# Retention outputs of a block in two TensorE visits instead of three, the last product in two halves, and one chunk's load ahead of a queue of stores

## The chip, the cores and the metric

One core of a Trainium2 chip runs the whole program. The metric is the time of one execution on the device in microseconds (us), lower is better; a second view is one profiled execution, whose trace gives every instruction's start and duration on TensorE (PE; its weight loads PEld), VectorE (DVE), ScalarE (ACT), GpSimd (POOL) and the DMA queue that SyncE issues (SP).

## The reference

Retention with a decay per head, and behind it a feed-forward layer with ELU:

```python
for t in range(S):                       # B, H, S, D = 4, 8, 768, 64
    state = gamma * state + einsum('bhd,bhe->bhde', k[:, :, t], v[:, :, t])
    y[:, :, t] = scale * einsum('bhd,bhde->bhe', q[:, :, t], state)
x = y.transpose(0, 2, 1, 3).reshape(B * S, H * D)        # 3072 x 512
h = x @ w_in                                             # 512 x 2048
out = where(h > 0, h, exp(min(h, 0)) - 1) @ w_out        # 2048 x 512
```

All of it is float32.

## The kernel before, in words

**Blocks and chunks.** The 3072 tokens are 24 chunks of 128, six to a sequence, and six blocks of 512 tokens (four chunks, two pairs of chunks). Block 0 (tb 0) is computed plainly, block 1 with Strassen's seven products once or twice, blocks 2 and 3 together and then 4 and 5 together ("big", `nb` 0 and 1) with two or three levels. The feed-forward layer of one group is on TensorE while the retention of the next is done between its products, in *visits*: `retention_step(tb, step)` is called at places written out by hand, steps 0 to 4 for a block. The schedule is manual: every engine runs its instructions in the order in which the program issues them.

**A block's retention.** Step 0 is `scores` of both pairs: k^T q in 64 x 64 matmuls (line 331), then a mask on DVE (line 342) into the chunk's tile. Step 1 is `states`: k^T v' (line 371), then a chain of running sums on DVE (line 383). Steps 2 to 4 are `outputs_step`, which drives one generator `outputs(tb, pp)` for each pair of chunks: `within` (line 427) is the masked scores times v', `across` (line 442) the state times q, both added up in PSUM tiles `y`; then DVE multiplies by the decay into x (line 417). `y` of a pair is two tiles of 512 columns, one for each half (64 tokens) of a chunk; a tile is written by matmuls from the lower and the upper 64 rows of the array. So that these do not overlap, DVE copies a few elements of it (`seen`, line 411) between `across(other=0)` and `across(other=1)`, and TensorE waits for that copy.

With two generators the three steps run: step 2, pair 0 as far as its `seen`; step 3, the end of pair 0 and pair 1 as far as its `seen`; step 4, the end of pair 1 (blocks 1 to 3). For blocks 4 and 5 the ends of both pairs are in step 4. Scores, k^T v' and `y` tiles share the four buffers of pool `ps_r`, each one PSUM bank.

**Where the visits are.** Block 1: between the plain products of block 0 (line 557). Block 2: in `first(3)` and `second_twice(1)` (lines 784 and 978). Block 3: pair 0's scores and states in `second_twice(1)`; pair 1's scores and states and the output steps in the first two of eight `big_twice` units of `nb` 0 (line 1286), in five visits. Blocks 4 and 5: in `second_big(0)` (line 1395), at the places of the list `VISITS`, named by (product number, "first", "middle" or "end").

**Loads and stores.** All DMAs are issued by SP in program order. A chunk is 1 MB, `load(m)` (line 125), into one of four buffers; `scale_v` (line 305) then multiplies v by the decay on POOL. Weights come through a ring of slots `wq` (line 854): `done` frees a slot behind the last product that read it and `fetch` issues the next loads of a long list; pieces named in `blocked` are held until `sent(j)`. Block 3's last chunk (15) is loaded at (5, "end") of `second_twice(1)`, behind six of eight stores of weight sums `xb` (line 679) that are issued from step 5 on; `sent(1)` follows at (6, "first").

**The last product.** `inner_end` (line 1435 on) is the seven small products of the last of seven; its product 3 adds onto the bank `pa` of products 1, 6 and 5, and a DVE add and one store (lines 1466 and 1467) end the program:

```python
            product(j, 3, pa, False)
            add(res[:, 0, 1], pa, k[:, 0, 1])
            nc.sync.dma_start(to[:, 0, 1], res[:, 0, 1])
```

Of the kernel before, what the change touches and what calls it, by code (L numbers as in the profile page):

```python
# [28 lines left out]
def kernel(  # L29
# [40 lines left out]
    C = P  # L70
# [376 lines left out]
    def outputs_of_first():  # L447

        y = [bank(x).rearrange("p a (b x d) -> p (a b) x d", b=2, x=2) for x in "bd"]
        for x in range(2):  # L450
# [19 lines left out]
            if not x:  # L470
                yield

    def outputs_step(tb, step):

        if step == 0:
            held["y"] = [outputs(tb, pp) for pp in range(2)]
        early_end = tb <= 3
        if step and early_end:
            next(held["y"][step - 1], None)
        elif step == 2:  # L480
            for g in held["y"]:
                next(g, None)
        if step < 2:
            next(held["y"][step])
            next(held["y"][step])

    half = [slice(0, TH), slice(TH, TB)]

# [356 lines left out]
    def sent(j):  # L845
        send_small()
        blocked.discard((2, "t", j))
        fetch()
# [531 lines left out]
    def second_big(nb, behind_last):  # L1380
        ts, kept2 = {}, {}
        ends = nb == NB - 1

        def input_parts(j):
            x = INPUT2[j]
            t = (slots_e, slots_s)[len(ts) % 2]
            b11, b12, b21, b22 = (quarter(x, a, b) for a in range(2) for b in range(2))
            yield from quarters_of(t, b11, b12, b21, b22, nc.gpsimd if j == 1 else nc.vector)
            ts[j] = {1: b11, 2: b21, 3: b22, 4: t[3], 5: t[0], 6: t[1], 7: t[2]}

        def product(j, k, ps, begin):
            name = (nb + 2, j, k)
            w = where[name].rearrange("p (f d) -> p f d", f=4)
            for f in range(4):
                nc.tensor.matmul(  # L1395
                    ps, lhsT=w[:, f, :], rhs=ts[j][k][:, f // 2, f % 2, :], start=(begin and f == 0), stop=(f == 3),
                    skip_group_check=True,
                )
            done(name)

        def copy(ps):
            m = small.tile([P, TH], FP32, name="ms", tag="ms")
            nc.scalar.copy(m, ps)  # L1403
            return m

        def add(o, x, y):
            nc.vector.tensor_tensor(out=o, in0=x, in1=y, op=ALU.add)  # L1407

        part = lambda x: bank(x)[:, 0]

        def inner(j):
            res = (two if j in (6, 7) else mpool).tile([P, 2, 2, TH], FP32, name="res", tag="m")
            pa = part("a")
            product(j, 1, pa, True)
            m1 = copy(pa)
            pb = part("b")
            product(j, 2, pb, True)
            add(res[:, 0, 0], pb, m1)
            yield
            product(j, 6, pa, False)  # L1420
            u2 = copy(pa)
            pd = part("d")
            product(j, 7, pd, True)
            yield
            product(j, 5, pa, False)
            add(res[:, 1, 1], pd, copy(pa))
            yield
            product(j, 3, pa, False)
            nc.scalar.copy(res[:, 0, 1], pa)  # L1429
            yield  # L1430
            product(j, 4, pd, False)
            add(res[:, 1, 0], pd, u2)
            sum_up(j, res.rearrange("p d t c -> p (d t c)"))

        def inner_end(j):

            res = mpool.tile([P, 2, 2, TH], FP32, name="res", tag="m")
            to = out_of[nb][1, 0].rearrange("p (d t c) -> p d t c", d=2, t=2)
            k = kept2[6].rearrange("p (d t c) -> p d t c", d=2, t=2)
            pa = part("a")  # L1440
            product(j, 1, pa, True)
            m1 = copy(pa)
            pb = part("b")
            product(j, 2, pb, True)
            add(res[:, 0, 0], pb, m1)
            yield
            product(j, 6, pa, False)
            u2 = copy(pa)
            pd = part("d")
            product(j, 7, pd, True)  # L1450
            m7 = copy(pd)
            yield
            add(u2, u2, k[:, 1, 0])
            add(u2, pd, u2)
            product(j, 5, pa, False)
            add(res[:, 1, 1], pa, m7)
            yield
            add(res[:, 0, 0], res[:, 0, 0], k[:, 0, 0])
            nc.sync.dma_start(to[:, 0, 0], res[:, 0, 0])
            add(res[:, 1, 1], res[:, 1, 1], k[:, 1, 1])  # L1460
            pb = part("b")
            product(j, 4, pb, True)
            add(res[:, 1, 0], pb, u2)
            nc.sync.dma_start(to[:, 1], res[:, 1])
            product(j, 3, pa, False)
            add(res[:, 0, 1], pa, k[:, 0, 1])
            nc.sync.dma_start(to[:, 0, 1], res[:, 0, 1])

        def store(name, h):
            nc.sync.dma_start(out_of[nb][int(name[1]) - 1, int(name[2]) - 1], h)  # L1470

        def sum_up(j, m):

            kept2[j] = m
            if j == 2:
                add(m, kept2[1], m)
                store("C11", m)
            elif j == 6:
                add(m, kept2[1], m)
            elif j == 5:  # L1480
                add(m, kept2[6], m)
                add(kept2[6], kept2[6], kept2[7])
                add(kept2[7], m, kept2[7])
                store("C22", kept2[7])
                add(kept2[3], m, kept2[3])
                store("C12", kept2[3])
            elif j == 4:
                add(m, kept2[6], m)
                store("C21", m)

        for _ in input_parts(1):
            yield "input"
        yield "inputs"
        before = iter(())
        changes = itertools.chain(*(next_big_input(x) for x in ("T3", "T2", "T1", "T4")))
        for at, j in enumerate(BIG2):
            cur = (inner_end if j == 4 and ends else inner)(j)
            next(cur)
            if j == 1:
                yield "tail"  # L1500
            for _ in before:
                pass
            if at:
                yield "first"
            some(changes, {2: 1, 3: 4, 7: 1, 5: 2}.get(j, 0))
            parts = input_parts(BIG2[at + 1]) if at + 1 < 7 else iter(())
            if j == 1:

                next(cur)
                yield "elu"  # L1510
                some(parts, 2)
            else:
                some(parts, 2)
                if at == 6:
                    behind_last()
                next(cur)
                yield "middle"
            next(cur)
            if j != 1:
                for _ in parts:  # L1520
                    pass
                some(changes, {2: 2, 6: 3, 7: 2}.get(j, 0))
            before = cur
            yield j
            if j == 1:
                for _ in parts:
                    pass
                some(changes, 1)
        for _ in before:
            yield "rest"  # L1530
# [267 lines left out]
    flush()  # L1798
    retention_step(2, 2)
    step, VISITS = 0, {(1, "first"): 3, (1, "end"): 4}  # L1800
    LOADS = {(1, "first"): 0, (1, "end"): 1, (3, "end"): 2, (5, "end"): 3}
    for s in sec:
        if s == "first":
            step += 1
        at = (step, s if s in ("first", "middle") else "end")
        if s in ORDER2 and 1 <= step <= 4:
            some(smalls[1], 1 if step < 4 else 3)
        if step == 5:
            send_small(2)
        elif at == (6, "first"):  # L1810
            sent(1)
        if at in VISITS:
            retention_step(2, VISITS[at])
        if at in LOADS:
            load(3 * CPB + LOADS[at])
            scale_v(3 * CPB + LOADS[at])
        if at == (3, "first"):
            scores(3, 0)
        elif at == (4, "first"):
            states(3, 0)  # L1820
        if s == ORDER2[-1]:
            break
    for _ in sec:
        pass
    mid.close()
# [5 lines left out]
    for nb in range(NB):  # L1831
# [83 lines left out]
        for at, (j, sub) in enumerate(ORDER1):  # L1915
# [18 lines left out]
            if nb == 0:  # L1934
                if at == 0:
                    scores(3, 1)
                elif at == 1:
                    retention_step(3, 3)
            if at == 7:
                run(tail)  # L1940
                seeds(0, 1, first=True)
            next(cur)
            tail = cur
            if nb == 0:
                if at == 0:
                    states(3, 1)
                elif at == 1:
                    retention_step(3, 4)
                    run(tail)
            side(at, 2)  # L1950
# [81 lines left out]
        if more:  # L2032
# [1 line left out]
                scale_v(groups[0] * CPB + n)  # L2034
        step = 0
        VISITS = [
            (0, "end"), (1, "end"), (2, "middle"), (2, "end"), (3, "middle"),
            (5, "first"), (5, "end"), (6, "first"), (6, "middle"), (6, "end"),
        ]
        LOADS = [(3, "middle"), (3, "end"), (4, "first"), (4, "middle")]  # L2040
# [70 lines left out]
```

## Time and profile before

| | us |
|---|---|
| three runs | 612.51, 608.03, 608.09 (median 608.09) |
| the profiled execution | 607.38 |
| its span from the first to the last instruction | 605.6 |
| PE busy in the span | 599.0 (99%) |
| PEld, DVE, ACT, POOL busy | 491.9, 508.6, 261.5, 98.3 |
| granted TensorE clock | 1.00 |
| DMA share of 16 engines | 70.9%, 139.85 MB |

The table is read from the top of the profile page and the run's times. The outputs' matmuls are line 427 (704 recorded into `y`, 12.7 us busy) and line 442 (592 and 64 recorded, 14.2 and 3.4 us busy); each matmul of the program is recorded as two. DVE multiplies `y` by the decay in 22 instructions of 0.68 us each (line 417).

### The profile page before, as it was taken

Reading aid. Unit: us, or ns where it says so; the run is one execution under the profiler, and the core shown is the slowest. Engines: PE = TensorE matmul, PEld = TensorE weight load, DVE = VectorE, ACT = ScalarE, POOL = GpSimd, SP = SyncE. Lnnn points to the kernel's source line nnn. Section 1 sums busy time; section 2 is a strip of 40 time slices with the busy share of each in tenths; the row PEclk is TensorE's granted clock in tenths of the full one; section 3 lists DMA queues with packets and bytes.
Section 4 is the critical chain, followed back from the end, with each engine's and each line's share of the span. In section 5 each row is a group of like instructions: output and inputs, shape, how many; then the busy total and the mean of one; then the engine's idle time right before and its main releaser. Section 6 shows DMA issues by size and latency. Waiting matters only on the chain.

```text
span 605.6 us, 13752 instructions
## 1 busy us (share of the span) xinstructions
PE 599.0 (99%) x5510; PEld 491.9 (81%) x5510; DVE 508.6 (84%) x779; ACT 261.5 (43%) x448; POOL 98.3 (16%) x77
## 2 busy tenths in 40 slices
PE   7999999999999999999999999999999999999997
PEld 5865568888889999888766888888888866888886
DVE  6778889989899886899898887898658999779785
ACT  6898734205543112247589210100236779611110
POOL 2020000000230110000797000120000398000000
PEclk9999999999999999999999999999999999999999
DMA  8797578789968998698976445874555676556552
GB/s 324 274 407 289 189 232 254 227 244 268 351 224 264 354 348 294 204 307 272 352 248 217 129 131 153 273 277 112 197 167 151 172 221 194 160 150 188 154 152 115
DMA packets 85680, 139.85 MB, mean 231 GB/s; under 512 B 6896, under 2 KB 46576, under 8 KB 80880
## 3 DMA queue, kind: packets, MB, share of 16 engines
q1 hardware_dynamic: 85616, 138.96, 70.9%
q8 instruction: 44, 0.72, 0.5%
q14 instruction: 20, 0.16, 0.1%
HBM read 105.12 MB, written 33.82 MB: 229 GB/s over the span
## 4 chain that ended last, share of the span: by engine, by line
PE 97%; DMA 1%; DVE 1%; issue 0%; SPq 0%; ACT 0%
PE pa L1395 16%; PE pa L1286 9%; PE pd L1395 8%; PE pa L784 5%; PE pd L1286 5%; PE x L1349 4%; PE pb L1395 4%; PE pa L978 4%; PE pa L557 3%; PE x L647 3%; PE pb L1286 2%; PE pd L784 2%; PE pa L647 2%; PE pa L1336 2%; PE sc L331 2%; PE kv L371 2%
## 5 line engine op out<-in xcount | busy, mean ns | idle before, releaser
L1403 ACT COPY ms<-pa 128x256 f32<-128x256 f32 x41 | 15.3, 372 | 106.5 <-PE pa L1395 103.5
L1395 PE MATMUL pa<-gC,wq 128*128 128x256 f32 x240 | 56.8, 381 | 0.0
L1395 PEld LDWEIGHTS pa<-gC,wq 128*128 128x128 f32 x240 | 45.1, 190 | 7.3 <-issue 1.0
L305 POOL TENSOR_TENSOR chunk<-chunk,vf 128x512 f32<-128x512 f32 x15 | 19.6, 1316 | 153.6 <-DMA chunk<-in_qkv_dram 104.7
L1362 ACT ACTIVATE r<-r 128x512 f32<-128x512 f32 x64 | 40.4, 631 | 2.0
L1407 DVE TENSOR_TENSOR res<-pd,ms 128x256 f32<-128x256 f32 x26 | 11.0, 422 | 28.2 <-PE pd L1395 17.5
L1297 ACT COPY m<-pa 128x512 f32<-128x512 f32 x32 | 18.7, 584 | 35.0 <-PE pa L1286 31.8
L1395 PE MATMUL pd<-w_all,wq 128*128 128x256 f32 x120 | 28.3, 379 | 0.0
L1363 DVE SCALAR_TENSOR_TENSOR gC<-r,gC 128x512 f32<-128x512 f32 x24 | 27.9, 1169 | 0.0
L926 POOL TENSOR_TENSOR wp<-wp 128x512 fp32r<-128x512 f32 x6 | 8.8, 1467 | 116.5 <-DMA scratch_dram<-wi 102.2
L183 ACT ACTIVATE w_all<-wraw 128x1024 uint32<-128x1024 uint32 (+1 forms) x19 | 19.2, 1009 | 15.1 <-PE x L647 9.6
L1395 PEld LDWEIGHTS pd<-w_all,wq 128*128 128x128 f32 x120 | 22.8, 190 | 3.1
L1857 POOL TENSOR_TENSOR chunk<-chunk,w_all 128x512 f32<-128x512 f32 x4 | 5.1, 1287 | 124.4 <-ACT w_all L1297 124.4
L1377 DVE TENSOR_TENSOR gC<-w_all,gC 128x1024 f32<-128x1024 f32 x20 | 24.2, 1260 | 0.0
L1349 PE MATMUL x<-xl,wq 128*128 128x512 f32 x64 | 23.7, 457 | 0.0
L1395 PE MATMUL pa<-w_all,wq 128*128 128x256 f32 x96 | 22.9, 381 | 0.0
L1395 PE MATMUL pa<-ts,wq 128*128 128x256 f32 x96 | 22.9, 381 | 0.0
L185 ACT ACTIVATE w_all<-wraw 128x1024 fp8e4<-128x1024 f32 (+1 forms) x19 | 22.6, 1190 | 0.6
L1395 PE MATMUL pd<-ts,wq 128*128 128x256 f32 x96 | 22.7, 379 | 0.0
L557 PE MATMUL pa<-xb,w_all 128*128 128x512 f32 x48 | 21.5, 597 | 0.0
L1429 ACT COPY res<-pa 128x256 f32<-128x256 f32 x13 | 4.8, 373 | 38.1 <-PE pa L1395 38.1
L213 DVE CUSTOM_DVE_ANT_0 w_all<-wraw,w_all 128x2048 uint16<-128x2048 uint16 (+1 forms) x19 | 20.1, 1059 | 0.8
(369 smaller groups left out, 1598.6 us busy)
## 6 DMA issues: line engine op xcount, KB each, us to landing
wq<-scratch_dram SPq DMA_DIRECT2D x231, 256.0 KB, 3.4
chunk<-in_qkv_dram SPq DMA_DIRECT2D x22, 1024.0 KB, 7.5
wraw<-in_w_dram SPq DMA_DIRECT2D x15, 1024.0 KB, 5.9
scratch_dram<-wp SPq DMA_DIRECT2D x8, 512.0 KB, 3.9
out_dram<-res SPq DMA_DIRECT2D x7, 512.0 KB, 3.4
scratch_dram<-gT SPq DMA_DIRECT2D x12, 256.0 KB, 3.6
wq<-scratch_dram SPq DMA_DIRECT2D x24, 128.0 KB, 2.9
scratch_dram<-w_all SPq DMA_DIRECT2D x12, 256.0 KB, 3.1
```

The source lines that it names most:

```text
L185: nc.scalar.activation(top, hi.bitcast(FP32), AF.Copy, scale=2.0**-120, saturate=False)
L213: vec.tensor_tensor(out=flat, in0=c, in1=flat, op=ALU.add)
L557: nc.tensor.matmul(hp, lhsT=w[n][:, fi, j // 2, j % 2, :], rhs=xb[:, j, :], start=(j == 0), stop=(j == 3))
L647: nc.tensor.matmul(X[j][:, d, :], lhsT=w[j][:, d * P : d * P + P], rhs=x[j], start=(n == 0 and d == 0), stop=at_end, skip_group_check=True,)
L784: nc.tensor.matmul(ps[:, fi, :], lhsT=w[:, fi, j2, :], rhs=x[:, j2, :], start=(begin and fi == 0 and j2 == 0), stop=(j2 == 1), skip_group_ ...
L978: nc.tensor.matmul(ps, lhsT=w[:, f, :], rhs=ts[j][k][:, f, :], start=(begin and f == 0), stop=(f == 3), skip_group_check=True,)
L1286: nc.tensor.matmul(ps[:, f, :], lhsT=w[:, f, :], rhs=big_xs[j][k], start=(begin and f == 0), stop=True, skip_group_check=True,)
L1349: nc.tensor.matmul(joined(ps), lhsT=where[name][:, c : c + P].bitcast(F32R), rhs=x[:, k], start=(not third and c == 0), stop=(k == 1), ski ...
L1362: nc.scalar.activation(r, r, AF.Exp, scale=-1.0)
L1363: return lambda: nc.vector.scalar_tensor_tensor(g, r, -1.0, h, ALU.add, ALU.max)
L1377: nc.vector.tensor_tensor(out=quarter(to, r, t), in0=quarter(x, r, t), in1=quarter(y, r, t), op=op)
L1395: nc.tensor.matmul(ps, lhsT=w[:, f, :], rhs=ts[j][k][:, f // 2, f % 2, :], start=(begin and f == 0), stop=(f == 3), skip_group_check=True,)
```

## The change

1. `outputs_of_block(tb)` takes the place of the two generators for blocks 1 to 5 (block 0 keeps `outputs`). It has four `y` tiles at once, one for each half `sub` and each row group `a`. Its first visit is all of `within` for four chunks and two `seen` copies; its second is all of `across` and the multiplications of the tiles with a = 0; its third has the multiplications with a = 1 only, and no matmul. In blocks 1 and 4, which cross from one sequence to the next, each multiplication is done in two halves.
2. For block 4 the second of these visits is at (3, "first") instead of (2, "end").
3. Block 3: chunk 15 is loaded at (5, "first"), ahead of the `xb` stores, which start at step 6; `sent(1)` comes behind the loop. Scores and states of pair 1 are in one visit, and both later output steps in one place.
4. `inner_end`: product 3 is done in two halves of 128 columns in fresh banks, each with its own add and store; what `pa` holds before is added to the result by one more DVE add.

```diff
+    def outputs_of_block(tb):
+        y = [[ps_r.tile([P, 2, 4, D], FP32, name="y", tag="r") for _ in range(2)] for _ in range(2)]
+        ms = [raw[tb * CPB + n] for n in range(CPB)]
+        for n in range(CPB):
+            for u in range(2):
+                for a in range(2):
+                    pt = ms[n // 2 * 2 + a][0][:, 1].rearrange("p h c -> p (h c)")
+                    for c in range(2):
+                        for sub in range(2):
+                            nc.tensor.matmul(
+                                y[sub][a][rows(c), u, n, :], lhsT=ms[n][1][rows(sub), 0, head(a, u, c), :],
+                                rhs=pt[rows(sub), (n % 2 * HP + 2 * u + c) * D :][:, 0:D],
+                                start=(n == 0 and u == 0), stop=False, skip_group_check=True,
+                            )
+        for sub in range(2):
+            seen = epool.tile([P, 8], FP32, name="seen", tag="seen")
+            nc.vector.tensor_copy(seen.rearrange("p (u n) -> p u n", u=2), y[sub][1 - sub][:, :, :, 0])
+        yield
+        for n in range(CPB):
+            for other in range(2):
+                for u in range(2):
+                    for a in range(2):
+                        sub = a ^ other
+                        if fresh(tb, 2 * n + sub):
+                            continue
+                        for c in range(2):
+                            p = 2 * u + c
+                            nc.tensor.matmul(
+                                y[sub][a][rows(c), u, n, :], lhsT=state(tb, 2 * n + sub)[rows(a), p, :],
+                                rhs=ms[n][0][rows(a), 0, p, rows(sub)], start=False, stop=True, skip_group_check=True,
+                            )
+        at = [chunks[tb * CPB + n][1] for n in range(CPB)]
+        runs = [slice(0, CPB)] if at[2] == at[0] + 2 else [slice(0, 2), slice(2, CPB)]
+        for a in range(2):
+            for sub in range(2):
+                for r in runs:
+                    i = at[r.start]
+                    nc.vector.tensor_tensor(
+                        out=of_sub(x_of(tb)[:, 2 * a : 2 * a + 2, r.start * C : r.stop * C], sub), in0=y[sub][a][:, :, r],
+                        in1=of_sub(etab[:, a, :, i * C : (i + r.stop - r.start) * C], sub), op=ALU.mult,
+                    )
+            if not a:
+                yield
...
     def outputs_step(tb, step):
         if step == 0:
-            held["y"] = [outputs(tb, pp) for pp in range(2)]
-        early_end = tb <= 3
-        if step and early_end:
-            next(held["y"][step - 1], None)
-        elif step == 2:
-            for g in held["y"]:
-                next(g, None)
-        if step < 2:
-            next(held["y"][step])
-            next(held["y"][step])
+            held["y"] = outputs_of_block(tb)
+        next(held["y"], None)
...
             add(res[:, 1, 1], pa, m7)
+            add(res[:, 0, 1], pa, k[:, 0, 1])
...
-            product(j, 3, pa, False)
-            add(res[:, 0, 1], pa, k[:, 0, 1])
-            nc.sync.dma_start(to[:, 0, 1], res[:, 0, 1])
+            for x, c in (("a", slice(0, P)), ("d", slice(P, TH))):
+                ps = part(x)[:, 0:P]
+                product(j, 3, ps, True, c, x == "d")
+                add(res[:, 0, 1, c], ps, res[:, 0, 1, c])
+                nc.sync.dma_start(to[:, 0, 1, c], res[:, 0, 1, c])
...
-    LOADS = {(1, "first"): 0, (1, "end"): 1, (3, "end"): 2, (5, "end"): 3}
+    LOADS = {(1, "first"): 0, (1, "end"): 1, (3, "end"): 2, (5, "first"): 3}
...
-        if step == 5:
+        if step == 6:
             send_small(2)
-        elif at == (6, "first"):
-            sent(1)
...
         if s == ORDER2[-1]:
             break
+    sent(1)
...
             if nb == 0:
                 if at == 0:
                     scores(3, 1)
-                elif at == 1:
-                    retention_step(3, 3)
+                    states(3, 1)
...
             if nb == 0:
-                if at == 0:
-                    states(3, 1)
-                elif at == 1:
+                if at == 1:
+                    retention_step(3, 3)
                     retention_step(3, 4)
                     run(tail)
...
-            (0, "end"), (1, "end"), (2, "middle"), (2, "end"), (3, "middle"),
+            (0, "end"), (1, "end"), (2, "middle"), (3, "first"), (3, "middle"),
```

`product` in `second_big` takes two more arguments for this, the columns and whether the weights' slot may be freed behind it.

More of the change, by code (lines that the diff above doesn't have):

```diff
@@ L473, in outputs_step @@
+    of_sub = lambda t, sub: t.rearrange("p u (n s c) -> p u n s c", s=2, c=D)[:, :, :, sub]
     def outputs_step(tb, step):
         if step == 0:
-            held["y"] = [outputs(tb, pp) for pp in range(2)]
-        early_end = tb <= 3
-        if step and early_end:
-            next(held["y"][step - 1], None)
-        elif step == 2:
-            for g in held["y"]:
-                next(g, None)
-        if step < 2:
-            next(held["y"][step])
-            next(held["y"][step])
+            held["y"] = outputs_of_block(tb)
+        next(held["y"], None)
@@ L1389, in input_parts, with product @@
             ts[j] = {1: b11, 2: b21, 3: b22, 4: t[3], 5: t[0], 6: t[1], 7: t[2]}
-        def product(j, k, ps, begin):
+        def product(j, k, ps, begin, columns=slice(0, TH), last=True):
             name = (nb + 2, j, k)
@@ L1395, in product @@
                 nc.tensor.matmul(
-                    ps, lhsT=w[:, f, :], rhs=ts[j][k][:, f // 2, f % 2, :], start=(begin and f == 0), stop=(f == 3),
+                    ps, lhsT=w[:, f, :], rhs=ts[j][k][:, f // 2, f % 2, columns], start=(begin and f == 0), stop=(f == 3),
                     skip_group_check=True,
                 )
-            done(name)
+            if last:
+                done(name)
         def copy(ps):
```

## The prediction

> **What bounds the kernel now.** First the page's busy shares and the shares of the chain that ended last:
>
> ```profile
> PE 599.0 (99%) x5510; PEld 491.9 (81%) x5510; DVE 508.6 (84%) x779; ACT 261.5 (43%) x448; POOL 98.3 (16%) x77
> ...
> PE 97%; DMA 1%; DVE 1%; issue 0%; SPq 0%; ACT 0%
> ```
>
> TensorE carries 97% of the chain, so time is won by making its queue shorter and lost where it is made to wait. The list of waits says that its matmuls hardly wait: past the first instruction no entry adds up to more than 0.5 us. So I read its timeline, start to start, where the 64 x 64 visits are. Columns: start, length, engine, line, operation, count of recorded instructions (two to a matmul of the program). First scores alone (128 in block 5, 64 in block 3), then block 5's three output visits, then the end of DVE's run ahead of them:
>
> ```profile
> 210.59 1.16 PE L331 MATMUL sc<-chunk 64*64 64x64 f32 x64
> 211.68 1.16 PE L978 MATMUL pa<-ts,wq 128*128 128x128 f32 x8
> ...
> 402.77 2.10 PE L331 MATMUL sc<-chunk 64*64 64x64 f32 x128
> 404.79 1.99 PE L1395 MATMUL pa<-ts,wq 128*128 128x256 f32 x8
> 406.62 1.89 PE L1395 MATMUL pd<-ts,wq 128*128 128x256 f32 x8
> ...
> 419.29 1.16 PE L427 MATMUL y<-chunk 64*64 64x64 f32 x64
> ...
> 420.84 1.99 PE L1395 MATMUL pa<-gC,wq 128*128 128x256 f32 x8
> 422.67 1.89 PE L1395 MATMUL pd<-w_all,wq 128*128 128x256 f32 x8
> 424.49 1.16 PE L427 MATMUL y<-chunk 64*64 64x64 f32 x64
> 425.48 0.65 PE L442 MATMUL y<-chunk 64*64 64x64 f32 x32
> 426.05 1.99 PE L1395 MATMUL pa<-gC,wq 128*128 128x256 f32 x8
> ...
> 429.07 1.13 PE L1286 MATMUL pa<-xt,wq 128*128 128x256 f32 x4
> ```
>
> ```profile
> 419.92 4.88 DVE L1407 TENSOR_TENSOR res<-res 128x1024 f32<-128x1024 f32 x4
> 424.72 0.23 DVE L411 COPY seen<-y 128x8 f32<-128x8 f32 x2
> ```
>
> ```profile
> 600.57 1.94 PE L1395 MATMUL pa<-gC,wq 128*128 128x256 f32 x8
> 602.55 0.43 DVE L1407 TENSOR_TENSOR res<-pa,res 128x256 f32<-128x256 f32 x1 [1.08 <-PE pa L1395]
> 603.00 0.33 SPq L1467 DMA_DIRECT2D out_dram<-res  x1
> ```
>
> The reader is to see what a visit costs beside its matmuls. 64 recorded instructions take 211.68 - 210.59 = 1.09 us, 128 take 2.02 (the other visits of 128: 2.03). That is 0.15 us fixed and 14.7 ns an instruction. The product behind a visit takes 406.62 - 404.79 = 1.83 us where the same shape in a row takes 1.73 (0.10 more); the product ahead takes 0.09 more (422.67 to 424.49 is 1.82). So a visit costs 0.34 us beside its instructions.
>
> The Trainium skill (Perfetto Trace Analysis, Identifying the Most-Contended Engine) says that matmul busy time is a poor measure of TensorE's headroom. The trace bears on it: by PE's 99% the idle time in these visits is nearly nothing and a merged visit would win about 0; start to start it wins 0.34. I go by start to start.
>
> **Part 1 and 2: outputs in two visits.** Instructions stay the same in number and shape; only their grouping changes. New visits hold 128 (`within`) and 112 or 128 (`across`, 112 where a sequence begins in the block), so 2.03 and 1.80 or 2.03. `within` now cycles the halves inside the columns, `across` has the same cycle; scores alternate the same way as the first and cost the same per instruction, and block 5's visits of `across` alone (64, 1.09 us) cost as the second. Per block, old visits against new, and 0.19 for the two edges of the visit that is gone:
> - block 1: 1.56 + 2.03 + 0.61 = 4.20 against 3.83: -0.37, -0.19: **-0.56**
> - block 2: 1.56 + 2.03 + 0.63 = 4.22 against 4.06: **-0.35**
> - block 4: 1.56 + 1.56 + 1.08 = 4.20 against 3.83: **-0.56**
> - block 5: 1.55 + 1.56 + 1.09 = 4.20 against 4.06: **-0.33**
>
> Added waits, each read at its place. All four `y` banks are now wanted at once, so the first visit waits for the last running sum of k^T v', too, not for half of them. Those sums end on DVE 1.8 us ahead of the visit in block 1 (67.0 against 68.8), 4.8 in block 2, 4.6 in block 4, 2.4 in block 5. No wait. `seen` is now behind all of `within`, and all of `across` waits for it: in blocks 1 to 4 at least one product of 1.7 us or more and DVE's queue lie between. Tight is block 5: DVE's four sums of 1.22 us begin when the product ahead of the visit ends, so `seen` ends at 424.95 as before; TensorE comes at 419.29 + 2.03 + 3.65 = 424.97, and a hand-over from DVE to PE took 0.06 at the start of the trace (`seen` ends 8.41, matmul 8.47). I take 0.04, bounds 0 and 0.5 (half of one 1.22 sum late).
>
> DVE: two `seen` of 0.15 go in each block; eight multiplications of 256 columns (0.42, spaced 0.34) for four of 512 (0.68, spaced 0.61) add some 0.2 us in blocks 1 and 4. The multiplications with a = 0 now wait for all of `across`: in block 1 until about 76.3, where DVE before was at work from 74.8; but the a = 1 ones are ready when reached, where DVE idled 1.99 us at 78.4, so it comes out about 0.3 us earlier at the next work, TensorE 0.56 earlier. DVE then is busy with half a us of gaps from 80.4 to 127.8; the tightest hand-over I find there (inputs `xb` ending 88.2, used at 89.8) has 1.6 us. It covers the difference of 0.25. In block 4 the multiplications move around 377 to 384, end within 0.2 us of before, and the next DVE step still waits for ACT's copy, as before. I cost these at 0; if that cover is gone, it is 0.2 to 0.3 us a block.
>
> **Part 3: block 3.** Old: scores 1.28 (0.19 above the fit: the chunk lands while they run; POOL begins on it at 241.01, first thing), k^T v' 1.09, outputs 1.56 + 2.01 + 0.63: 6.57. New: 2.03 + 2.03 + 1.80 = 5.86, -0.71. Two visits' edges: -0.38. Together **-1.09**. The load is moved past six stores and three weight loads on SP: issued at about 228.6 for 233.07, so with the 7.9 us it took it lands at 236.5 and POOL (1.04) has v' by 237.6; the matmuls want it at about 240.3 less what was won. The running sums then end at about 244.5 on DVE, the output visit comes at 245.1: 0.6 us of cover, the least of all blocks; bounds of a wait 0 and 0.6.
>
> The eight `xb` stores and what is behind them in SP's queue move back. Before, they went out at 228.6 to 237.7. Now they begin behind the store that went at 235.34; eight of 0.45 us with three small weight loads between them take to about 242, as a ring waits 5.7 us for each store's landing. The first weights of unit 3 follow at about 243, land (3.4) at 246.3, wanted at 258.2. The piece after waits for two more stores, about 247.4, then SP has caught up with the wait for a slot that held it until 250.9 before. Cover about 11 us. Cost 0, bounds 0 and what R2 prices.
>
> **Part 4: the end.** Product 3 in two halves of 128 columns: the row of line 978 has 0.893 us for eight recorded of that shape, so 1.79 for 1.73: +0.06. DVE's last add is 128 wide: 0.28 (line 990's rows) for 0.43: -0.15. The new add (0.42) comes while product 4 and 3 run and delays the store of 256 KB by 0.35, to about 601.85; it lands in 2.0, at 603.9, ahead of the last. The last store is 64 KB: 128 KB landed in 1.7 and 256 KB in 2.0, an estimate of 1.6 by that slope. Bounds 0 and -0.3, I take -0.1. Sum **-0.2**.
>
> The Trainium skill (DMA: Bandwidth & Descriptors, Anatomy of one DMA) gives a fixed 2 us or so for a transfer, whatever its size, for the software path. The 1.7 us here is under it. By that rule the halved store wins nothing and the sum would be 0.1 less.
>
> **The sum.** -0.56 - 0.35 - 1.09 - 0.56 - 0.33 - 0.2 + 0.04 = -3.05 us, against the profiled execution's 607.38: 604.3. The three runs' median stands 0.7 above the profiled execution, and I carry that over: 608.09 - 3.05 = 605.0.
>
> **The rivals.**
> R1, the waits come back: TensorE finds `y` banks or `seen` late in blocks 3 and 5 and DVE's 0.2 to 0.3 in blocks 1 and 4, in all 0.6 + 0.5 + 0.5 = 1.6. For it: the 0.6 and 0.02 us of cover. Against: everywhere else the cover is over 1.5 us. Time 606.6.
> R2, slower: the later `xb` stores make the weights of unit 3 late. Price: each us past 258.2 is a us on the path, and the pieces behind come in the same queue. For it: SP issues in order, and a store took up to 5.7 us to land. Against: 11 us of cover, so it decides only where the stores' landing is 11 us longer, and 3 us more eats the gain; with 16 us longer the time is 608.09 - 3.05 + 5 = 610.0.
> R3, the regrouping does not make the visits cheaper: the 0.34 was not a switch, but belongs to the matmuls (their order, the banks they add to), and only scores' 0.19 and the end remain: 607.7. Against: visits of 32, 64, 96 and 128 all lie on one line.
> R4, more comes off than the line gives: a visit of 88 in block 4 (1.56) lies 0.12 over it, as does one of 120 in block 1 (2.03), and both change from one kind to the other inside. The ten new visits have no such change; if 0.1 of each goes, the time is 604.0.
>
> **How the numbers follow.** Forecast 0.68, R1 0.13, R2 0.06, R3 0.06, R4 0.07. Range: low 603.8 (R4 and the end's bound of 0.2 more), high 607.3 (R1 with the same 0.7); R2 and half of R3 are left out. About 1%, 6 us, is what a measurement of this kernel can tell from no change. Only R2 at its far end reaches that on the slow side (0.04); faster by over 6 us would take twice the sum (0.02). The rest, 0.94, is within 1%.
>
> **What would show it.** Right: each block's outputs are two stretches on PE, of 2.0 and 1.8 to 2.0 us, with no wait on DVE at the second; block 3's scores and k^T v' take 2.0 together; POOL's scaling of chunk 15 ends near 238; the last add is 0.28. Wrong: `y` waiting on DVE line 383 in block 3 or on `seen` in block 5 (R1), a product of unit 3 waiting on a weight load (R2), stretches of 128 that take over 2.3 (R3).

## The result and the profile after

The changed kernel took 606.37 us (median of 20 runs, 605.44 to 607.96) and the kernel before, beside it, 609.66 (20 runs, 607.74 to 613.1): ratio 0.9951, 95% interval 0.9938 to 0.9964. A second time it was 606.67 against 608.82, 0.9954 (0.9932 to 0.9976). By the ratios that is 3.0 and 2.8 us, near the forecast's -3.05 and within 1%; the medians themselves differ by 3.3 the first time and by 2.15 the second. The two profiled executions say something else: 607.58 after (span 605.8) against 607.38 before (605.6). The profile of before was of an execution faster than any of its 125 timed runs (607.52 to 613.51); that of after was one of its slower ones. So what follows compares stages, not spans.

The busy line and the shares of the chain, in the page of the changed kernel:

```profile
PE 598.2 (99%) x5518; PEld 492.7 (81%) x5518; DVE 508.3 (84%) x779; ACT 261.8 (43%) x448; POOL 99.1 (16%) x77
...
PE 94%; DVE 3%; DMA 2%; issue 1%; ACT 0%; SPq 0%; DVEq 0%; ACTq 0%
```

PE's busy time fell by 0.8 us, far less than the stretches below won, and its share of the chain fell from 97% to 94%: other engines now release it here and there. The list of waits names them (engine, line and tile, what it waited for: sum, times, longest):

```profile
PE pa L1017 <- DMA wq<-scratch_dram: 0.9, 1, 0.9
...
PE pd L1017 <- DVE res L1029: 0.5, 1, 0.5
...
PE pa L1325 <- ACT m L1336: 0.4, 1, 0.4
```

Block 5's outputs in the timeline of the changed kernel (the first 32 instructions of `across`, from 425.83, are listed in small groups and left out):

```profile
420.15 2.10 PE L483 MATMUL y<-chunk 64*64 64x64 f32 x128
422.18 2.00 PE L1434 MATMUL pa<-gC,wq 128*128 128x256 f32 x8
...
426.34 1.58 PE L501 MATMUL y<-chunk 64*64 64x64 f32 x96
427.85 2.00 PE L1434 MATMUL pa<-gC,wq 128*128 128x256 f32 x8
```

Two visits of 2.03 and 2.02 (425.83 to 427.85), and no wait on `seen`. The end of the program:

```profile
602.76 0.95 SPq L1510 DMA_DIRECT2D out_dram<-res  x2
603.06 0.29 DVE L1447 TENSOR_TENSOR res<-pd,res 128x128 f32<-128x128 f32 x1 [0.56 <-PE pd L1434]
```

Now all kernels by stage. A stage runs from one visit's first matmul to another's, read from PE's timeline, so it holds every wait inside it: "start" to block 1's scores; "b1" on to block 2's scores; "b2" to the first scores of block 3; "w" (no visit changed, but the place of the loads and stores) to its second; "b3" to the first 512-column product behind it; "f" a stretch of such products; "b4" to block 5's scores; "b5" to the second `second_big`; "end" to the end of the span.

```
              start     b1     b2      w     b3      f     b4      b5   end   span
before        57.50 114.53  38.56  29.67  51.66  37.65  73.20  114.92  87.9  605.6
before_again  58.32 114.53  38.56  29.68  53.23  40.24  73.20  114.89  87.9  610.6
end           57.73 114.52  38.56  29.95  51.61  37.68  73.20  114.92  87.6  605.8
load          58.14 114.53  38.56  30.86  51.76  37.67  73.20  114.94  87.9  607.6
blk3          58.23 114.53  38.77  30.52  52.06  37.67  73.20  114.90  87.9  607.8
outs          58.31 114.31  38.20  30.07  51.86  37.66  72.68  114.53  87.9  605.5
noload        58.25 114.01  38.21  30.06  52.49  37.65  72.68  114.55  87.6  605.5
after         58.19 114.45  38.39  31.25  51.00  37.67  72.68  114.57  87.6  605.8
again         57.63 114.02  38.37  30.50  51.86  37.66  72.69  114.57  87.6  604.9
mid           58.24 114.01  38.21  30.06  51.28  37.67  72.69  114.57  87.6  604.3
late_stores   58.28 114.72  38.29  30.36  50.81  37.68  72.68  114.56  87.6  605.0
split         58.31 115.20  38.56  30.07  51.02  37.65  72.99  114.91  87.6  606.3
tight         58.16 114.03  38.56  30.07  51.26  37.68  72.69  115.21  87.6  605.3
tight14       59.02 114.02  38.29  29.37  50.52  37.64  72.69  114.53  87.6  603.7
```

Where nothing waits, a stage repeats to 0.05 us (f, b4 and b5 in most rows). The start differs by up to 1.5 with the code the same, and before's first profile has the shortest.

### The profile page after: what moved, and what is told of

It is laid out like the page before. It is cut to its first block, busy times and chain, and to the rows that moved or that the text cites. A ratio compares the mean times of both kernels' runs of the same rounds, so it can differ in the third digit from the quotient of the medians.

```text
span 605.8 us, 13774 instructions
## 1 busy us (share of the span) xinstructions
PE 598.2 (99%) x5518; PEld 492.7 (81%) x5518; DVE 508.3 (84%) x779; ACT 261.8 (43%) x448; POOL 99.1 (16%) x77
## 4 chain that ended last, share of the span: by engine, by line
PE 94%; DVE 3%; DMA 2%; issue 1%; ACT 0%; SPq 0%; DVEq 0%; ACTq 0%
PE pa L1434 16%; PE pa L1325 8%; PE pd L1434 8%; PE pa L823 5%; PE x L1388 4%; PE pb L1434 4%; PE pd L1325 4%; PE pa L596 3%; PE x L686 3%; PE pa L1017 3%; PE pd L823 2%; PE pa L686 2%; PE pa L1375 2%; PE sc L331 2%; PE pb L1325 2%; PE kv L371 2%
## 5 line engine op out<-in xcount | busy, mean ns | idle before, releaser
L1434 PE MATMUL pa<-gC,wq 128*128 128x256 f32 (+1 forms) x240 | 55.6, 378 | 0.0
```

What stands on the lines that cost most here:

```text
L1434: nc.tensor.matmul(ps, lhsT=w[:, f, :], rhs=ts[j][k][:, f // 2, f % 2, columns], start=(begin and f == 0), stop=(f == 3), skip_group_check ...
```

## The experiments

The theory (T1): each part pays what its stretches say, visits and their edges. Rivals: the early load takes block 3's gain back by delaying weights (T2); or the early load itself wins most of the timed gain, because chunk 15 comes late in other executions of before (T3).

**outs, blk3, end, load: one part each, on the kernel before.** `outs` is `outputs_of_block` with block 4's visit at (3, "first"). `load` and `blk3`:

```diff
-    LOADS = {(1, "first"): 0, (1, "end"): 1, (3, "end"): 2, (5, "end"): 3}
+    LOADS = {(1, "first"): 0, (1, "end"): 1, (3, "end"): 2, (5, "first"): 3}
-        if step == 5:
+        if step == 6:
             send_small(2)
-        elif at == (6, "first"):
-            sent(1)
...
+    sent(1)          # blk3 has, besides: states(3, 1) right behind scores(3, 1)
```

`end` is the change to `inner_end` and `product`.

> The kernel before with parts 1 and 2 alone: outputs of blocks 1 to 5 in two visits; block 3's load, scores and k^T v' and the end as before. T1 (every part pays what the stretches of its visits say): blocks 1, 2, 4 and 5 win 0.53 + 0.35 + 0.51 + 0.35 = 1.75 us by start to start, block 3's three output visits of 1.56 + 2.01 + 0.63 become two of about 3.9 with one edge of 0.19 less, another 0.5: together -2.2 us, ratio near 0.9963. T2 (block 3's part nets nothing, so outputs and end carry all of the measured -3.3): -3.0, ratio 0.995. T3 (the earlier load carries much of the timed gain): -1 or less, ratio 0.998 to 1.

> The kernel before with block 3's part alone: chunk 15 loaded ahead of the stores, the stores from step 6, scores and k^T v' of pair 1 in one visit; outputs with the two generators as before, the end as before. T1: the scores' 0.19, a visit's 0.15 and its edges of 0.19 less, -0.5 us, ratio 0.9991. T2: the profile after has a wait of 0.95 us for the weights of the last product of second_twice(1), whose load went out 0.5 us behind the chunk's, and 0.4 us on ScalarE's copy; they take this back and more: 0 to +0.9, ratio 1.000 to 1.0015. T3: -1 or more, ratio under 0.9985, since chunk 15 landed late in some executions of before.

> The kernel before with part 4 alone: product 3 in two halves in fresh banks, each with its add and store. T1 and T2: -0.2 to -0.3 us, ratio 0.9995 to 0.9997. The rule that a transfer costs the same whatever its size: -0.1. T3: the same. In the profile the last add is 0.29 us for 0.43 and the end of the span comes 0.2 to 0.3 us earlier behind the last whole product.

> The kernel before with only the order of SP's queue changed: chunk 15 loaded at (5, first), the stores of xb from step 6, the release behind them; all visits as before. T1: 0 to -0.2 us (the scores of block 3 need no longer wait for the chunk). T2: the weights of the last product of second_twice(1) come 0.9 to 1.1 us late behind the chunk, and a copy on ScalarE 0.4 us late behind a store: +1.0 to +1.5 us, ratio 1.0016 to 1.0025. T3: -1 us or more, ratio under 0.9985.

Measured: outs 0.9976 (0.9964 to 0.9989), blk3 0.9997 (0.9984 to 1.0009), end 1.0003 (0.9983 to 1.0023), load 0.9999 (0.9982 to 1.0017). Only outs is told from 1, by 1.5 us; the parts add up to -1.5 and the whole is -3.0. The intervals are wide enough for that gap (0.7 to 1.2 us each side), but the stages say more. In b1, b2, b4 and b5 outs wins 0.22, 0.36, 0.52 and 0.39, about T1's but for b1's 0.22 (0.53 was expected; the wait behind it is shown under "Block 1" below). In b3 it wins nothing (51.86 against 51.66) although a visit has gone there too. load and blk3 lose 1.19 and 0.85 in w; 0.80 of the first and all of the second are T2's mechanism: PE waits for the weights of `second_twice(1)`'s last product, whose load now stands behind the chunk's. The changed kernel, PE and SP's queue:

```profile
235.68 1.06 PE L1017 MATMUL pb<-w_all,wq 128*128 128x128 f32 x8
237.69 1.13 PE L1017 MATMUL pa<-gC,wq 128*128 128x128 f32 x8 [0.95 <-DMA wq<-scratch_dram]
```

```profile
229.43 0.42 SPq L125 DMA_DIRECT2D chunk<-in_qkv_dram  x1
229.94 2.71 SPq L893 DMA_DIRECT2D wq<-scratch_dram  x4
```

This wait is in four of the five profiles with the load at (5, "first"), 0.95 (after), 0.61 (blk3), 0.55 (load) and 0.20 (again; split, below, has none), and in no profile with the load elsewhere. It goes with the time that the chunk ahead took to land: 7.0, 7.1 and 6.9 us in after, blk3 and load, 5.9 and 6.1 in again and split. The rest of load's loss in w, 0.38, is a wait on DVE near 226.5, taken up with tight14 below.

T3 is not borne out: the load alone won nothing in b3, and its ratio is 0.9999 where T3 asked for under 0.9985, which its interval just reaches. Nor did it rid the kernel of long executions: 3 of load's 12 took over 610 us (36 of 125 of before); of outs and noload, which load the chunk as before, none of 24.

**again, noload, mid, late_stores: the changed kernel, and its load put elsewhere.** noload undoes the whole block of the diff shown above (load, stores and release) and keeps the merged visit; the others change one key:

```diff
-    LOADS = {(1, "first"): 0, (1, "end"): 1, (3, "end"): 2, (5, "first"): 3}
+    LOADS = {(1, "first"): 0, (1, "end"): 1, (3, "end"): 2, (5, "middle"): 3}   # mid
+    LOADS = {(1, "first"): 0, (1, "end"): 1, (3, "end"): 2, (5, "end"): 3}      # late_stores
```

> The changed kernel itself once more, on the chip of the three runs below. By outs, blk3 and end alone (0.9976, 0.9997, 1.0003) the parts add up to -1.5 us, where the whole gave 0.9951, -3.0. If the parts simply add up and the two intervals only overlap: ratio 0.995 to 0.9975. In its profile the wait for the weights of the last product of second_twice(1) comes back, 0.5 to 1 us, as in every profile so far with the chunk's load ahead of the stores (0.95, 0.61, 0.55) and in none without it.

> The changed kernel with SP's queue as before (chunk 15 at (5, end), stores from step 5, release at (6, first)); visits and end as changed. T1 (the wait for the weights is paid): it goes, 0.6 to 1.1 us off in the profile; but scores and k^T v' of pair 1 now come in one visit behind a chunk that lands about 240.9, POOL's v' 1.04 later, at 242: k^T v' would be wanted at 240.9 + 1.0 and waits 0 to 0.5. Net 0.3 to 1.0 below the changed kernel, ratio near 0.994. T2 (the early load nets nothing): the same as the changed kernel, 0.995. T3 (the early load wins much): 1 us or more above it, 0.9965 or more.

> The changed kernel with chunk 15 loaded one place later, at (5, middle), so that SP issues two loads of weights ahead of it; the stores stay behind. T1: the weights of the last product no longer stand behind 1 MB, its wait of 0.55 to 0.95 us goes, the chunk lands 2 us later, near 238.5, v' at 239.6, still ahead of the scores at 241: 0.5 to 1 us below the changed kernel, ratio 0.9935 to 0.9945. T2 and T3: within 0.3 of the changed kernel.

> The changed kernel with chunk 15's load back at (5, end), the stores still from step 6. No store is then ahead of the chunk, and it goes out near 231 to 232, behind the weights. T1: no wait for weights; the chunk lands near 239.5, v' at 240.6, about as the scores begin: as mid, 0.5 to 1 us below the changed kernel; the 0.3 to 0.4 us on ScalarE's copy at 258 stays. T2 and T3: within 0.3 of the changed kernel or above.

Measured: again 0.9954 (0.9932 to 0.9976), noload 0.9971 (0.9952 to 0.9990), mid 0.9955 (0.9935 to 0.9975), late_stores 0.9949 (0.9931 to 0.9967). The intervals overlap, so no order of the four is shown by time (medians 606.67, 607.31, 606.25, 605.84); noload's 0.9971 is where T3 put it, but its interval reaches down to 0.9952. The stages are clear. noload's w has no wait for weights, but its b3 is the longest of all with merged visits: TensorE comes to the scores of pair 1 earlier than before, and the chunk does not.

```profile
240.53 0.69 PE L331 MATMUL sc<-chunk 64*64 64x64 f32 x32
242.16 0.69 PE L331 MATMUL sc<-chunk 64*64 64x64 f32 x32 [0.93 <-DMA chunk<-in_qkv_dram]
242.68 1.30 PE L371 MATMUL kv<-chunk 64*64 64x64 f32 x64
```

So T1's 0 to 0.5 for the cost of the late chunk was too low, and T1 and T2 were wrong to treat the parts as separate: the early load wins nothing alone, yet without it what blocks 1 and 2 win is waited away at the chunk (0.93, and 0.19 more in k^T v'). mid keeps the early chunk and clears the weights; the product that waited 0.95 starts without one:

```profile
235.11 1.06 PE L1017 MATMUL pb<-w_all,wq 128*128 128x128 f32 x8
236.00 1.06 PE L1017 MATMUL pa<-gC,wq 128*128 128x128 f32 x8
```

In late_stores, b1 is 0.71 longer than in mid (the wait behind that is shown under "Block 1" below), and another weight came 0.79 late, at 227.2; its b3 has no wait.

What is left in b3 is a wait near 258 that no profile of before has: 0.40 in after, 0.28 in outs, 0.54 in noload, 1.01 in again. ScalarE's part of it, and SP's, in again:

```profile
255.96 0.58 ACT L1336 COPY gC<-pa 128x512 f32<-128x512 f32 x1 [3.95 <-PE pa L1325]
257.50 0.63 ACT L963 ACTIVATE wp<-w_all 128x512 fp32r<-128x512 f32 x1 [0.96 <-DMA scratch_dram<-wp]
258.04 0.57 ACT L1336 COPY m<-pa 128x512 f32<-128x512 f32 x1
```

```profile
243.70 7.59 SPq L893 DMA_DIRECT2D wq<-scratch_dram  x3
251.34 0.94 SPq L718 DMA_DIRECT2D scratch_dram<-wp  x2
```

ScalarE's next write of `wp` waits until the store of the last one has landed, and the copy that TensorE needs is queued behind that write. SP issues the store (two pieces, at 251.3 and 251.9) behind weight loads that wait until TensorE has freed a slot (250.5). From the store's issue to that write it was 6.1 us in before (250.95 to 257.04); in again ScalarE was free for it 5.2 us behind (256.54), since TensorE's way there is shorter by what the merged visits won. The store's second piece takes 4.9 to 5.5 us in these four profiles. That is where outs lost part of its gain in b3, with the stores still early.

**split, tight, tight14, before_again.** split adds a visit; tight and tight14 are built on mid.

```diff
         for n in range(CPB):                                # split, in across
+            if n == 2:
+                yield
...
-            if not a:
-                yield
```

```diff
-            if units and (at, place) in ((0, 2), (1, 2)):   # tight and tight14
+            if units and (at, place) in ((0, 2), (2, 0)):
...
+    LOADS = {(1, "first"): 0, (1, "end"): 1, (4, "first"): 2, (5, "middle"): 3}   # tight14
```

> The changed kernel with one visit more in blocks 1, 2, 4 and 5: across is cut after its second chunk, the second half comes a product or two later, and all multiplications of a block follow it. Block 3 has both halves in one place. If a visit costs 0.15 us fixed and 0.19 at its edges, TensorE loses 4 x 0.34 = 1.36 us, readable in each block from the starts of the products around it; ratio to before about 0.9975 where the changed kernel had 0.9951 and 0.9954. If the gain was not the number of visits but what is inside them (order of the matmuls, four banks), it loses nothing there: 0.995. A loss over 2 us would be DVE's multiplications coming later, and would show as waits of TensorE on DVE.

> As mid, and ScalarE's write of wp that follows the store of the first wp is issued one product later, at place (2, 0) for (1, 2), behind the copy that TensorE waits for. Theory W: TensorE's wait for that copy near 258 us (0.40, 1.01, 0.54 and 0.28 in four profiles with the output visits merged, none before the change) is the store's landing: the weight slot that lets SP go on is freed before block 3's visits, and the store takes 4.9 us from there, so what the visits won behind that point is partly waited away. With the write moved, the wait is gone in any execution: 0 in the profile, and 0.2 to 0.6 us below mid's 0.9955, near 0.995. If the wait has another cause it comes back, on the same copy. The write of wp itself then ends 1 to 2 us later, and DVE's two steps on it: no wait expected there.

> As tight, and chunk 14 is loaded a product or two later, at (4, first). In most profiles POOL's scaling of this chunk runs while DVE does the sums that TensorE waits for at 226 to 227 us (one DVE step of 0.68 us takes 1.53 beside it, TensorE waits 0.46). If that is the cause, the scaling moves to 225.5 or later, the steps at 222 to 226 take their 0.68, and the wait at 226.5 is 0 to 0.1: 0.3 to 0.4 us below tight. Against it: 1 MB now goes out in the midst of weight loads, and one of them may come late, as in late_stores (0.79): then nothing is won.

> The kernel before itself, for a second profile and as a measure of the comparison: ratio 1.000 within 0.0015. Its first profiled execution, 607.38, was among its fastest (607.5 to 613.5 over 90 runs). Theory: its slower executions wait in block 3 for chunk 15, which goes out behind six stores (0.19 us in the first profile, 0.93 where the visits ahead of it were shortened and the load left where it was), and in its startup (0.2 to 0.8 us in all other profiles). Then a second profile that is slower by x shows these two as most of x. Against: x lies in stretches that wait for nothing the profile shows.

Measured: split 0.9991 (0.9974 to 1.0007), tight 0.9955 (0.9936 to 0.9975), tight14 0.9940 (0.9919 to 0.9961), before_again 1.0006 (0.9986 to 1.0026).

split gives the visit's price back: against mid, b2, b4 and b5 are 0.35, 0.30 and 0.34 longer, for 0.34 expected, though its matmuls, their order and their banks are those of the changed kernel, and no matmul of these three stages waits for DVE's later multiplications. (b1 is 1.19 longer: 0.34 and a DVE that comes later; TensorE waits 0.28 for its line 670, which had itself waited for a store of `gT` to land.) By time split is 2.4 us behind the changed kernel, and these four stages add up to 2.2. Block 4's cut, in its timeline:

```profile
377.78 0.65 PE L503 MATMUL y<-chunk 64*64 64x64 f32 x32
378.36 1.99 PE L1434 MATMUL pa<-ts,wq 128*128 128x256 f32 x8
380.19 1.89 PE L1434 MATMUL pd<-ts,wq 128*128 128x256 f32 x8
382.01 0.94 PE L503 MATMUL y<-chunk 64*64 64x64 f32 x48
```

The two products between the halves take 1.83 and 1.82 for 1.73: the edges again.

tight has no wait near 258, but neither had mid, whose store landed in 3.8 us; and 0.61 came up at 278, where mid waited 0.48 and split 0.23 for a weight. In tight the list names ScalarE for it, but the weight's load landed 0.13 us before the product began, as in mid and split. Its b5 holds another 0.40, block 5's scores waiting for their chunk. By time it is mid. That the store's landing sets the wait is seen in the four profiles above; that the move removes it for good is not shown.

tight14 takes away the wait at 226.5, 0.46 in all but one of the other profiles with merged outputs. In the changed kernel DVE's add and POOL's scaling of chunk 14 run at the same time:

```profile
225.56 1.53 DVE L920 TENSOR_TENSOR xb<-w_all,xb 128x512 f32<-128x512 f32 x1
227.01 0.28 DVE L1029 TENSOR_TENSOR res<-pb,ms 128x128 f32<-128x128 f32 x1
```

```profile
225.06 1.48 POOL L305 TENSOR_TENSOR chunk<-chunk,vf 128x512 f32<-128x512 f32 x1 [13.28 <-DMA chunk<-in_qkv_dram]
```

In tight14 the chunk comes later and POOL collides with a step that nobody waits for; the add takes 0.68:

```profile
225.85 0.68 DVE L920 TENSOR_TENSOR xb<-w_all,xb 128x512 f32<-128x512 f32 x1
...
229.10 1.53 DVE L984 TENSOR_TENSOR w_all<-gC 128x512 f32<-128x512 f32 x1
```

```profile
228.60 1.48 POOL L305 TENSOR_TENSOR chunk<-chunk,vf 128x512 f32<-128x512 f32 x1 [17.87 <-DVE h L1029]
```

Stage w is 29.37, 0.69 under mid's and 0.30 under before's, and b3, now with no wait at all, 50.52. Its six runs lie between 605.01 and 605.87 (median 605.56); of the 32 of the changed kernel three are that low. By the intervals it is not told from the changed kernel; it is the lowest median measured.

before_again fell on an execution of 612.35. Its stages are the same as before's to 0.03 but for three: 0.82 at the start, 1.57 in b3 and 2.59 in f. The start and the chunk, which were expected to be most of it, are 2.4 of 5.0. b3's is the chunk, issued 5.4 us behind the first of the stores ahead of it in SP's queue (4.5 in the first profile):

```profile
229.42 0.93 SPq L679 DMA_DIRECT2D scratch_dram<-xb  x2
...
234.87 0.48 SPq L125 DMA_DIRECT2D chunk<-in_qkv_dram  x1
```

```profile
241.09 0.69 PE L331 MATMUL sc<-chunk 64*64 64x64 f32 x32
243.25 0.69 PE L331 MATMUL sc<-chunk 64*64 64x64 f32 x32 [1.47 <-DMA chunk<-in_qkv_dram]
```

In f, a weight came 0.40 late and three products then waited for DVE line 918, 0.78 in all; for the rest of the 2.59 the profile shows no cause, and whether it follows from the chunk stays open. Of before's 125 runs 36 took over 610 us; of the changed kernel's 32 none took over 609.

## Why the prediction was right, step by step

**The price of a visit: right.** Undisturbed, b1, b2, b4 and b5 won 0.52, 0.35, 0.52 and 0.35 for 0.56, 0.35, 0.56 and 0.33. Blocks 1 and 4 came out 0.04 short. b2 reached its 0.35 in outs, noload and mid, and 0.17 to 0.27 in after, again, late_stores and tight14; in tight it won nothing, and there one product behind the visit took 1.26 for 0.89. split paid 0.30 to 0.35 for 0.34. R3 is out, by split above all; R4 is out too, b1 and b4 gave less, not more.

**Block 3: the size right, the cover wrong.** The merged stretch won 1.14 where nothing disturbs it (tight14, 51.66 to 50.52, for -1.09). Scores and k^T v' take 2.03 (242.28 to 244.31), POOL's scaling of chunk 15 ended at 237.5, forecast 237.6. The output visit did not wait for the running sums, which had 0.6 us of cover.

**The step that failed is "Cost 0" for SP's queue.** I followed the stores to unit 3's weights, found 11 us of cover, and that held: no product of unit 3 waited for a weight in any profile. But of what the 1 MB load was moved past I priced the chunk's gain and not the three weight loads now behind it. They cost 0 to 0.95. (The 5.7 us that R2 calls the most a store took is the median of those eight; the longest took 6.7.) The second miss, ScalarE's write of `wp` (0.28 to 1.01), came not from the later stores: outs has it without them. A time that was enough before was made shorter by the very gain.

**Block 1: the cover that went was not DVE's 0.25.** b1 won 0.50 to 0.52 in again, mid, noload, tight and tight14, but 0.22 in outs, 0.08 in after, and lost 0.19 in late_stores. In these three DVE's first step on the tile `m` near 93 us waits 0.70, 0.75 and 1.08 for the landing of a store that reads `m`; in the other five it waits 0 to 0.38, in before not at all. The step in after, and in mid:

```profile
93.28 0.56 DVE L722 TENSOR_TENSOR m<-w_all 128x384 f32<-128x384 f32 x1 [0.75 <-DMA scratch_dram<-m]
```

```profile
92.50 0.55 DVE L722 TENSOR_TENSOR m<-w_all 128x384 f32<-128x384 f32 x1
```

DVE's later steps follow: in after those at 149 us end half a us later than in mid, and two products there take 1.88 and 1.83 for 1.73. Counted from block 1's scores, DVE is at this step at 34.9 us in before and at 34.3 in mid, earlier by what the visits won: again a store's landing has lost its cover. Why the store takes 6.4 us in mid and 6.8 to 7.2 in the three is open. So R1, which priced DVE's own work in blocks 1 and 4 and the banks in 3 and 5, did not come true: no `y` and no `seen` was late.

**The end: 0.3 for 0.2.** The adds won 0.14, the two halves cost 0.06, and from the last store's issue to the end of the span it is 2.4 (603.38 to 605.8) for 2.6. The last 64 KB landed 1.58 us behind its issue, before's last 128 KB 1.70, and the 256 KB of both 2.0. The Trainium skill (DMA: Bandwidth & Descriptors, Anatomy of one DMA) gives, for the software path, a fixed part of about 2 us and on top of it a part that grows with the size, by which 64 KB less is an estimate of 0.15 us. The trace agrees on the second part with 0.12; the fixed part is lower here. The prediction read only the fixed part, so "wins nothing", and the same rule in what was expected of end, is not what that section gives.

**The sum: the right size, in part by luck.** Stage gains that hold are 0.52 + 0.35 + 0.52 + 0.35 + 0.3 = 2.04. Block 3's 1.14 is mostly given back in w and b3 of the same profiles. Over all runs the medians are 2.2 apart (608.78 of before's 125, 606.54 of the changed kernel's 32), the lowest 2.1 (607.52 and 605.44): close to the 2.04, and 0.8 short of the forecast. The first comparison had long runs of before beside it (median 609.66 in those 20; 608.82, 608.82 and 608.37 in the other three sets), and the second one's interval reaches from 1.5 to 4.1 us. One long execution of before shows chunk 15 late (1.47 for 0.19), but since load alone keeps the long executions and outs and noload have none, the early load is not shown to relieve them; what does stays open.

**The level.** 606.37 lies 1.4 above 605.0 and inside the range. Half of that is the level: the median of before is 608.78 over 125 runs, not the 608.09 of three. The other half is what the sum had too much.

## What to carry to other kernels

Where a stretch is cut out of the bound engine's queue, look for every wait that was hidden by just that stretch: what is released before it and needed behind it (a store's landing, a load that starts at a fixed point) has now less cover. When a large load is moved ahead in an in-order queue, price the small urgent loads that it passes; one place further back was enough in the three profiles that have it (mid, tight, tight14). Judge sub-us parts by stages between the same instructions, since one profiled execution can be the fastest or the slowest of its kernel.

## What the hardware showed

Two vector engines at once cost more than expected: a DVE add of two SBUF tiles takes 1.53 us in place of 0.68 when POOL multiplies two at that time, and POOL's 1.04 becomes 1.48 (after). In the run `end` POOL began first, at 222.75, and took its 1.04; a DVE step begun at 222.93 took 1.41 for 0.68. The Trainium skill (SBUF — State Buffer, SBUF: two separate sides) says that the two share a pair of ports under an exclusive lock and the loser blocks; the trace agrees, with 0.85 and 0.73 lost by DVE, less than POOL's whole 1.04, which had begun earlier. Which of DVE's steps it hits decides: TensorE waited 0.46 behind the one at 225.6 and not at all behind the one at 229.1. And a visit can stall on no visible cause: in blk3 the first output visit of block 3 stopped 0.46 us in its midst with nothing named as releaser, and in again the first output visit of block 3 took 2.28 for 2.03.
